# Copies and additions that free PSUM banks go first at the borders of blocks, two groups of weight sums are issued a step earlier, and v gets four places

## The chip, the cores and the metric

The kernel runs on one core of a Trainium2 chip. The metric is the device time of one execution in microseconds. Engines are named as in the profile: PE (TensorE, matmuls), ACT (ScalarE), DVE (VectorE), POOL (GpSimd) and SP (SyncE, which issues the DMAs). Each engine works through its own instructions in the order in which they were issued, and an instruction that waits holds back all behind it on that engine.

## The reference

```python
scores = scale * np.matmul(q_c, k_c.transpose(0, 1, 2, 4, 3))     # chunks of 64 tokens, heads of 64
attn = softmax(scores); x = np.matmul(attn, v_c)                  # 4608 tokens x 512
h = x @ w_in                                                      # MoE 1: 512 -> 2048
x = (h * (1.0 / (1.0 + np.exp(-h)))) @ w_out                      # 2048 -> 512
h = x @ w_in2                                                     # MoE 2: 512 -> 1024
solu = h * softmax(h)
ln = (solu - mean(solu)) / np.sqrt(var(solu) + 1e-06) * g_ln
out = ln @ w_out2                                                 # 1024 -> 512
```

## The kernel before

The 4608 tokens are worked in nine blocks of 512 (b = 0 to 8). All matmuls are in fp16; each fp32 value is carried as a high and a low half. `split` makes them: the high half on ACT (L113), the low half on DVE (L118) or POOL (L117). A product of two such values takes three matmuls.

Blocks 0 and 1 multiply plainly. From block 2 on (FAST = 2) a product of two matrices is done with seven products instead of eight, over sums of quarters: `h_fast` is the first product of MoE 1, `x_fast` the second, `m_fast` the first of MoE 2. All three run through `combine`, which holds partial results in PSUM (tiles pa, pb, pc) and moves them out: the copy of j = 0 on ACT (L529, into h[0], which is called hc, xc or e by the user), of j = 3 (L533), of j = 1 (L536), and additions on DVE (L569: j = 4 from pc, j = 2 from pa, j = 6 from pb). The last product (j = 5) goes into pa again, once the addition of j = 2 has read it. `h_fast` runs two halves, i = 0 and 1, interleaved, then two more, i = 2 and 3. There are eight PSUM banks, which all tiles share: a tile's first matmul waits until the last reader of the bank's former tile is done.

The sums of weights that the seven products need are made while blocks 1 and 2 run: `w1_sums` and `w2_sums` in block 1, `w3_sums` in block 2. A group is eight matmuls into wq, two ACT copies (L420, L421), four DVE sums (L423 to L426) and four splits on ACT and POOL into the staging tile ws; those of w1 and w2 go to DRAM by SP.

The order of the work around is set by hand. `step(s)` puts between the eight parts of a block's second product what the next block's attention needs: scores of one tile in steps 0, 1, 3 and 4, the product with v in steps 3 to 6, and groups of weight sums in the steps that W2F (w2's four groups, block 1) and W3S (w3's two groups, block 2) name. Attention of a tile is: qk loaded, split into qbh, qbl and kb (high halves on ACT), scores s_ps, maximum am, exponentials ae, transposed weights pT by DMA, v split into vbh and vbl, product x_ps, copy xf (L342).

At a border of blocks, `m_norm` makes the input u of the last product from e: exponentials (L799, L801), squares (L807), scaling (L817), u's high half on ACT (L818) and its low half on DVE (L821). This runs beside the next block's `h_fast`. In `combine` the list `behind` already puts a few instructions behind the copy L536 of i = 1:

```python
                i = A.activation(h[1], a, AF.Copy).ins
                while before:
                    tc.add_manual_dep(before.pop(), i.name, ORDERED, reason="copy first")
```

Of the kernel before, what the change touches and what calls it, by code (L numbers as in the profile page):

```python
# [46 lines left out]
def fused(ctx: ExitStack, tc: tile.TileContext, qkv, w1, w2, w3, w4, g_ln, out):  # L47
# [16 lines left out]
    MO = (0, 1, 2, 3)  # L64
    W3S = [0, 3]
    W1F = [3, 5, 7, 9, 11, 13, 14, 15]
    W2F = [3, 1, 7, 3]
    EXB = [6, 7, 10, 13, 14]
# [115 lines left out]
    def load_v(t):  # L184
        if t is not None:
            n = ORDER.index(t % TPB) if t // TPB > FAST else 0
            tag = ("vs", "h4", "h5", "h6")[n]
            vs[t] = one.tile([P, 512], F32, tag=tag, name="vs")
            nc.sync.dma_start(out=vs[t], in_=qkv[t, :, 2])

    def prep_qk(t, eng_l=G, ahead=True):
        q_, k_ = (y.rearrange("p (s i) -> p s i", s=NS) for y in qk.pop(t))
        qbh, qbl = qbs[t] if t in qbs else qb
        kb = one.tile([P, 2, NS, CH], F16, tag="xb2" if t in qbs else "k", name="kb")
        for r in (lo, hi):
            split(qbh[r, :, r], qbl[r, :, r], q_[r], 1.0, A, eng_l)
        split(kb[:, 0], kb[:, 1], k_, 1.0, A, V if t // TPB > FAST else eng_l)
        kt[t] = (qbh, qbl, kb[:, 0], kb[:, 1])
        if ahead and t % TPB != ORDER[-1]:
            load_qk(after(t))  # L200

    def prep_v(t):
        v = vs.pop(t).rearrange("p (s i) -> p s i", s=NS)
        vh, vl = vbh, vbl
        for r in (lo, hi):
            ready[1] = split(vh[r, :, r], vl[r, :, r], v[r], S_V, A, V)
        vt[t] = (vh, vl)
        if t // TPB <= FAST:
            load_v(after(t))
# [39 lines left out]
    def a_pv(t):  # L249
# [15 lines left out]
        if t % TPB != ORDER[-1]:  # L265
            prep_v(after(t))
        if o == ORDER[2]:
            v_done[:] = ready
        x_keep(b, o, ps.rearrange("p k c i -> p k (c i)"), S_X / (S_V * S_P))
        if sums_of and o == ORDER[2]:  # L270
            with tc.issue_after(v_done[0]), tc.issue_after(v_done[1]):
                sums_of.pop()()

    sums_of, v_done = [], [None, None]


# [57 lines left out]
    def x_keep(b, o, ps, scale):  # L334
# [5 lines left out]
        c = slice(o % 2 * P, o % 2 * P + P)  # L340
        f = one.tile([P, KD, P], F32, tag="h7" if o == ORDER[2] and b > FAST else f"h{o // 2}", name="xf")
        A.activation(f, ps, AF.Copy, scale=scale)  # L342
# [6 lines left out]
        split(xb[b, 2][:, 0, :, c], xb[b, 2][:, 1, :, c], f[:, 2:4], 1.0, A, G)  # L349
        if o == ORDER[1] and b > FAST:  # L350
            sums_of.append(lambda: x_sums(b, o, c, f))
        else:
            x_sums(b, o, c, f)

    def x_sums(b, o, c, f):
# [7 lines left out]
        for i in range(2):  # L363
            y = x.rearrange("p h t k n -> p h (t k) n")[:, :, 4 * i:4 * i + 4, c]
            split(y[:, 0], y[:, 1], t[i].rearrange("p t k n -> p (t k) n"), 1.0, A, V)


# [74 lines left out]
    def w1_sums(p):  # L442
# [3 lines left out]
        def staging():  # L446
# [4 lines left out]
             lambda j: w1s[p // 2][j, :, p % 2], [y[:, i] for i in range(4)], staging,  # L451
             y[:, 0::3].rearrange("p n a b -> p n (a b)"))

    def w2_sums(c, q):
# [61 lines left out]
    ORDERED = mybir.DependencyInfo(mybir.DependencyClass.NoSync, mybir.DependencyReason.DATA)  # L516
    behind = []

    def combine(h, shape, seq, product, done, add, c21_first=False, before=()):

# [5 lines left out]
        for j in seq:  # L526
            if j == 0:
                product(j, a, True)
                A.activation(h[0], a, AF.Copy)  # L529
            elif j == 3:  # L530
# [3 lines left out]
            elif j == 1:  # L534
                product(j, a, False)
                i = A.activation(h[1], a, AF.Copy).ins  # L536
                while before:
                    tc.add_manual_dep(before.pop(), i.name, ORDERED, reason="copy first")
            elif j == 4:
                p = bank(shape, "pc")  # L540
                product(j, p, True)
                add(0, h[0], p)
                done(0, 0, h[0])
# [24 lines left out]
    def plain_add(n, y, p):  # L568
        V.tensor_tensor(out=y, in0=p, in1=y, op=ALU.add)  # L569

# [8 lines left out]
    def h_fast(b, i):  # L579
# [7 lines left out]
        def done(r, c, x):  # L587
# [14 lines left out]
            else:  # L602
# [4 lines left out]
        yield from combine(h, [P, 2, HB], HSEQ, lambda *a: h_product(b, *a), done, plain_add,  # L607
                           before=behind if i == 1 else ())

# [14 lines left out]
    def x_fast(b, step, beside):  # L624
# [3 lines left out]
        def product(j, ps, start):  # L628
            step(XSEQ.index(j))
            if held:  # L630
                with tc.issue_after(v_done[0]), tc.issue_after(v_done[1]):
                    quarter(1, 1, held.pop())
# [91 lines left out]
    def m_fast(b, c, alt=False):  # L724
# [40 lines left out]

        yield from combine(y, [P, 512], XSEQ, product, done, add)
        u_tags, uT_tags = ["m1", "w3_10"], [tags[0] if c else "m2", tags[1]]
# [7 lines left out]
    def m_norm(b, ts, parts, m, es, u_tags, uT_tags, eng_l=V, defer=0):  # L775
# [39 lines left out]
        for i in range(n):  # L815
            e, u = es[i], us_[i]
            V.tensor_scalar(out=e, in0=e, scalar1=nmu[:, i:i + 1], scalar2=c[:, i:i + 1], op0=ALU.add, op1=ALU.mult)  # L817
            i_ = A.activation(u[:, 0, :], e, AF.Copy).ins  # L818
            if n > 1 and not defer and more_(b):
                behind.append(i_)  # L820
            eng_l.tensor_tensor(out=u[:, 1, :], in0=e, in1=u[:, 0, :], op=ALU.subtract)  # L821
            if isinstance(uT_tags[i], str):
# [144 lines left out]
    for b in range(NB):  # L967
# [46 lines left out]
        def step(s):  # L1014
# [10 lines left out]
            if b and s == 1:  # L1025
                run(m_out(b - 1, MO[TPB - 1]))
            for i in VL.get(s, ()) if b >= FAST else ():
                load_v(m + ORDER[i] if i < TPB else after(m + ORDER[-1]))
# [83 lines left out]
```

## Time and profile before

| | us |
|---|---|
| median of 3 runs | 1175.66 (1175.33 to 1175.7) |
| the profiled execution | 1176.06 |
| its span, first to last instruction | 1174.3 |
| PE busy | 1126.9 (96%) |
| DVE busy | 916.4 (78%) |
| ACT busy | 806.2 (69%) |
| POOL busy | 250.1 (21%) |

The profile is that of one execution. PE is busy almost all the time, the granted clock of its core is 0.991 of full speed, and the matmuls fill 1126.9 us. What can be changed without another set of matmuls is the time in which PE waits.

### The profile page before, as it was taken

Reading aid. Unit: us, or ns where it says so; the run is one execution under the profiler, and the core shown is the slowest. Engines: PE = TensorE matmul, PEld = TensorE weight load, DVE = VectorE, ACT = ScalarE, POOL = GpSimd, SP = SyncE. Lnnn points to the kernel's source line nnn. Section 1 sums busy time; section 2 is a strip of 40 time slices with the busy share of each in tenths; the row PEclk is TensorE's granted clock in tenths of the full one; section 3 lists DMA queues with packets and bytes.
Section 4 is the critical chain, followed back from the end, with each engine's and each line's share of the span. In section 5 each row is a group of like instructions: output and inputs, shape, how many; then the busy total and the mean of one; then the engine's idle time right before and its main releaser. Section 6 shows DMA issues by size and latency. Waiting matters only on the chain.

```text
span 1174.3 us, 23559 instructions
## 1 busy us (share of the span) xinstructions
PE 1126.9 (96%) x9036; PEld 769.2 (66%) x9036; DVE 916.4 (78%) x1638; ACT 806.2 (69%) x1475; POOL 250.1 (21%) x243
## 2 busy tenths in 40 slices
PE   6998898988999999999999999999999999999998
PEld 5444344444657866787678767876787777777853
DVE  5999998487588797789878986898689868886453
ACT  6887678766567767856875687568756876577253
POOL 2655434334201520031003100310021002100001
PEclk8999999999999999999999999999999999999999
DMA  6657579543446655776577567756776677565604
GB/s 261 224 179 208 152 232 270 163 140 112 143 127 203 197 151 144 189 233 180 154 189 234 171 153 198 225 171 162 187 218 181 162 176 217 175 162 145 204 21 116
DMA packets 205169, 209.18 MB, mean 178 GB/s; under 512 B 120192, under 2 KB 130432, under 8 KB 205056
## 3 DMA queue, kind: packets, MB, share of 16 engines
q1 hardware_dynamic: 205056, 207.68, 61.4%
q8 instruction: 70, 1.15, 0.4%
q14 instruction: 43, 0.35, 0.1%
HBM read 156.24 MB, written 24.12 MB: 154 GB/s over the span
## 4 chain that ended last, share of the span: by engine, by line
PE 61%; DVE 14%; ACT 11%; DMA 5%; issue 5%; POOL 3%; SPq 0%; ACTq 0%; POOLq 0%; DVEq 0%
PE o_ps L858 4%; PE o_ps L850 4%; PE o_ps L851 4%; PE pa L620 4%; PE pa L619 4%; PE pa L618 4%; PE pa L511 3%; PE pa L513 3%; PE pa L512 3%; PE pa L745 2%; PE pa L743 2%; PE pa L744 2%; DVE vbl L118 2%; PE pb L620 2%; PE pb L618 2%
## 5 line engine op out<-in xcount | busy, mean ns | idle before, releaser
L113 ACT ACTIVATE q<-hc 128x512 f16<-128x512 f32 x196 | 120.5, 627 | 43.1 <-DVE hc L598 16.0
L118 DVE SCALAR_TENSOR_TENSOR q<-hc,q 128x512 f16<-128x512 f32 x196 | 138.2, 721 | 10.9 <-ACT q L113 8.7
L117 POOL TENSOR_TENSOR qbl<-qk,qbh 64x512 f16<-64x512 f32 x54 | 71.4, 1322 | 265.7 <-ACT qbh L113 224.8
L618 PE MATMUL pa<-q,ring 128*128 128x256 f16 x448 | 122.1, 273 | 0.0
L620 PE MATMUL pa<-q,ring 128*128 128x256 f16 x448 | 122.1, 273 | 0.0
L619 PE MATMUL pa<-q,ring 128*128 128x256 f16 x448 | 122.1, 273 | 0.0
L850 PE MATMUL o_ps<-w4h,uT 128*128 128x512 f16 x288 | 109.1, 379 | 0.4 <-DVE e L801 0.4
L851 PE MATMUL o_ps<-w4l,uT 128*128 128x512 f16 x288 | 109.1, 379 | 0.0
L814 POOL TENSOR_TENSOR c<-c,mhalf 128x2 f32<-128x2 f32 (+1 forms) x22 | 14.1, 640 | 387.3 <-DVE c L813 377.4
L512 PEld LDWEIGHTS <-ring 128*128 128x128 f16 x784 | 76.7, 98 | 17.7 <-issue 7.4
L619 PEld LDWEIGHTS <-ring 128*128 128x128 f16 x784 | 76.7, 98 | 11.1
L618 PEld LDWEIGHTS <-ring 128*128 128x128 f16 x784 | 76.7, 98 | 11.1
L511 PEld LDWEIGHTS <-ring 128*128 128x128 f16 x784 | 76.7, 98 | 10.7 <-DMA ring<-w1s 0.4
L513 PEld LDWEIGHTS <-ring 128*128 128x128 f16 x784 | 76.7, 98 | 8.9
L620 PEld LDWEIGHTS <-ring 128*128 128x128 f16 x784 | 76.7, 98 | 8.9
L858 PE MATMUL o_ps<-w4h,uT 128*128 128x512 f16 x288 | 70.1, 379 | 0.0
L511 PE MATMUL pa<-xb,ring 128*128 128x256 f16 x224 | 61.0, 272 | 3.0 <-DVE hc L569 3.0
L511 PE MATMUL pa<-x,ring 128*128 128x256 f16 x224 | 61.0, 272 | 3.0 <-ACT hc L529 2.4
L511 PE MATMUL pb<-x,ring 128*128 128x256 f16 x224 | 61.1, 273 | 0.1
L618 PE MATMUL pb<-q,ring 128*128 128x256 f16 x224 | 61.1, 273 | 0.0
L619 PE MATMUL pb<-q,ring 128*128 128x256 f16 x224 | 61.1, 273 | 0.0
L620 PE MATMUL pb<-q,ring 128*128 128x256 f16 x224 | 61.1, 273 | 0.0
(277 smaller groups left out, 3490.8 us busy)
## 6 DMA issues: line engine op xcount, KB each, us to landing
ring<-w1s SPq DMA_DIRECT2D x196, 256.0 KB, 3.2
ring<-w2s SPq DMA_DIRECT2D x196, 256.0 KB, 3.7
wst<-w SPq DMA_DIRECT2D x48, 512.0 KB, 4.0
qk<-qkv SPq DMA_DIRECT2D x29, 512.0 KB, 4.1
vs<-qkv SPq DMA_DIRECT2D x36, 256.0 KB, 3.1
out<-o SPq DMA_DIRECT2D x36, 256.0 KB, 2.3
w1s<-ws SPq DMA_DIRECT2D x32, 128.0 KB, 2.1
w2s<-ws SPq DMA_DIRECT2D x16, 256.0 KB, 2.0
```

The lines of the kernel that those rows point to most:

```text
L113: ready[0] = A.activation(dst_h, src, AF.Copy, scale=scale).ins
L117: return G.tensor_tensor(out=dst_l, in0=src, in1=dst_h, op=ALU.subtract).ins
L118: return V.scalar_tensor_tensor(out=dst_l, in0=src, scalar=scale, in1=dst_h, op0=ALU.mult, op1=ALU.subtract).ins
L511: T.matmul(ps[:, c], wh, x[:, 0, k], start=first, stop=False, skip_group_check=True)
L512: T.matmul(ps[:, c], wh, x[:, 1, k], start=False, stop=False, skip_group_check=True)
L513: T.matmul(ps[:, c], wl, x[:, 0, k], start=False, stop=k == 1, skip_group_check=True)
L618: T.matmul(ps[:, c], wh, g[:, 0], start=first, stop=False, skip_group_check=True)
L619: T.matmul(ps[:, c], wh, g[:, 1], start=False, stop=False, skip_group_check=True)
L620: T.matmul(ps[:, c], wl, g[:, 0], start=False, stop=q == 1 and f == 3, skip_group_check=True)
L850: T.matmul(ps, uh[:, k], w4h[:, k, :], start=k == 0, stop=False)
L851: T.matmul(ps, uh[:, k], w4l[:, k, :], start=False, stop=False)
L858: T.matmul(ps, ul[:, k], w4h[:, k, :], start=False, stop=k == K2 - 1)
```

## The change

It adds no operation and takes none away; it moves some in their engines' order.

1. W3S: the second group of w3's sums is issued in step 2 of block 2 rather than in step 3. W2F: of the two groups of w2's sums in step 3 of block 1, one is issued in step 2.
2. The tiles of v that block 1 loads use four places (vs, h4, h5, h6) instead of one, and are loaded at the steps in VL. The sums of block 2's own x are put behind v's splits, as in later blocks.
3. `behind` becomes five lists. "keys": the last staging copy of w1's sums goes behind kb's high half. "first" and "second": in block 2, instructions of m_norm for block 1 go behind the copies L529 and L536 of i = 1. "sum": u's low halves go behind the addition L569 of j = 4, i = 1, at all borders. "joined": from block 3 on the high halves of the last tile's x differences go behind the copy of e from pa (L529) in `m_fast`.

```diff
-    W3S = [0, 3]
+    W3S = [0, 2]
-    W2F = [3, 1, 7, 3]
+    W2F = [2, 1, 7, 3]
...
-            n = ORDER.index(t % TPB) if t // TPB > FAST else 0
+            n = ORDER.index(t % TPB) if t // TPB >= FAST else 0
...
         split(kb[:, 0], kb[:, 1], k_, 1.0, A, V if t // TPB > FAST else eng_l)
+        put_behind("keys", ready[0])
...
             split(y[:, 0], y[:, 1], t[i].rearrange("p t k n -> p (t k) n"), 1.0, A, V)
+            if o == ORDER[3] and b > FAST:
+                behind["joined"].append(ready[0])
...
+        if p == 7:
+            behind["keys"].append(ready[0])
...
-    behind = []
-
-    def combine(h, shape, seq, product, done, add, c21_first=False, before=()):
+    behind = {n: [] for n in ("first", "second", "sum", "joined", "keys")}
+
+    def put_behind(name, i):
+        while behind.get(name):
+            tc.add_manual_dep(behind[name].pop(), i.name, ORDERED, reason="put behind")
+
+    def combine(h, shape, seq, product, done, add, c21_first=False, names=(None, None, None)):
...
-                A.activation(h[0], a, AF.Copy)
+                put_behind(names[0], A.activation(h[0], a, AF.Copy).ins)
...
-                i = A.activation(h[1], a, AF.Copy).ins
-                while before:
-                    tc.add_manual_dep(before.pop(), i.name, ORDERED, reason="copy first")
+                put_behind(names[1], A.activation(h[1], a, AF.Copy).ins)
...
-                add(0, h[0], p)
+                i = add(0, h[0], p)
+                if names[2]:
+                    put_behind(names[2], i)
...
-                           before=behind if i == 1 else ())
+                           names=("first", "second", "sum") if i % 2 else (None, None, None))
...
-        yield from combine(y, [P, 512], XSEQ, product, done, add)
+        yield from combine(y, [P, 512], XSEQ, product, done, add, names=(None if c else "joined", None, None))
...
-            i_ = A.activation(u[:, 0, :], e, AF.Copy).ins
+            high = A.activation(u[:, 0, :], e, AF.Copy).ins
+            low = eng_l.tensor_tensor(out=u[:, 1, :], in0=e, in1=u[:, 0, :], op=ALU.subtract).ins
             if n > 1 and not defer and more_(b):
-                behind.append(i_)
-            eng_l.tensor_tensor(out=u[:, 1, :], in0=e, in1=u[:, 0, :], op=ALU.subtract)
+                behind["second"].append(high)
+                behind["sum"].append(low)
+            elif n == 1 and b == FAST - 1 and ts[0] == 1:
+                behind["first"].extend(exps[-np:])
+                behind["second"].append(high)
+                behind["sum"].append(low)
+            elif n == 1 and b == FAST - 1 and ts[0] != 2:
+                behind["first"].append(high)
...
-            for i in VL.get(s, ()) if b >= FAST else ():
+            for i in VL.get(s, ()) if b >= FAST - 1 else ():
```

The order of instructions shows what this moves. Lines of the changed kernel carry higher numbers there: L585 is L569 of before, L606 is L590 (silu), L834 and L835 are L818 and L821. The numbers behind names tell tiles apart; hc0 of i = 0 is hc0_8486, of i = 1 hc0_8506.

DVE at one of the borders between blocks from 2 on, before:

```order
L569 TENSOR_TENSOR hc0_8486<-pc_8588,hc0_8486 128x512
L821 TENSOR_TENSOR u_8453<-e_8328,u_8453 128x1024
L821 TENSOR_TENSOR u_8454<-e_8329,u_8454 128x1024
L569 TENSOR_TENSOR hc0_8506<-pc_8607,hc0_8506 128x512
L118 SCALAR_TENSOR_TENSOR q_8418<-hc0_8486,q_8418 128x512
L569 TENSOR_TENSOR hc3_8489<-pa_8490,hc3_8489 128x512
L569 TENSOR_TENSOR hc3_8509<-pa_8510,hc3_8509 128x512
```

and after the change:

```order
L585 TENSOR_TENSOR hc0_8486<-pc_8588,hc0_8486 128x512
L585 TENSOR_TENSOR hc0_8506<-pc_8607,hc0_8506 128x512
L835 TENSOR_TENSOR u_8453<-e_8328,u_8453 128x1024
L835 TENSOR_TENSOR u_8454<-e_8329,u_8454 128x1024
L118 SCALAR_TENSOR_TENSOR q_8418<-hc0_8486,q_8418 128x512
L118 SCALAR_TENSOR_TENSOR q_8418<-hc0_8506,q_8418 128x512
L585 TENSOR_TENSOR hc3_8489<-pa_8490,hc3_8489 128x512
```

The second addition from pc now stands ahead of u's two low halves, and the low half of q for i = 1 ahead of the two additions from pa.

ACT at the same border, from the loading of the table for silu (L590), before:

```order
L590 ACT_TABLE_LOAD
L590 ACTIVATE hc0_8486<-hc0_8486 128x512
L113 ACTIVATE q_8418<-hc0_8486 128x512
L590 ACTIVATE hc0_8506<-hc0_8506 128x512
L113 ACTIVATE q_8418<-hc0_8506 128x512
L590 ACTIVATE hc3_8489<-hc3_8489 128x512
```

and after:

```order
L606 ACT_TABLE_LOAD
L606 ACTIVATE hc0_8486<-hc0_8486 128x512
L606 ACTIVATE hc0_8506<-hc0_8506 128x512
L113 ACTIVATE q_8418<-hc0_8486 128x512
L113 ACTIVATE q_8418<-hc0_8506 128x512
L606 ACTIVATE hc3_8489<-hc3_8489 128x512
```

The silu of i = 1 now stands ahead of the high half of q for i = 0.

ACT in block 2 at steps 2 to 4, behind the exponentials of step 1's tile (xc1 is x_fast's copy of j = 1, vbh the split of v), before:

```order
L113 ACTIVATE x2q_4510<-xc0_4216 128x2x128
L536 ACTIVATE xc1_4217<-pa_4220 128x512
L113 ACTIVATE qbh_113<-qk_4443 64x8x64 x2
L228 ACTIVATE ae_4600,as_4601<-s_ps_4573,am_4598 128x64 x8
L113 ACTIVATE kb_4611<-qk_4443 128x512
L113 ACTIVATE vbh_115<-vs_4394 64x8x64 x2
L342 ACTIVATE xf_4659<-x_ps_4630 128x512
```

and after:

```order
L430 ACTIVATE y_4515<-wq_4517 128x512
L113 ACTIVATE x2q_4510<-xc0_4216 128x2x128
L431 ACTIVATE y_4516<-wq_4518 128x512
L113 ACTIVATE w3s_4277<-y_4516 128x512
L113 ACTIVATE w3s_4278<-y_4516 128x512
L113 ACTIVATE w3s_4276<-y_4515 128x512
L113 ACTIVATE w3s_4279<-y_4515 128x512
L552 ACTIVATE xc1_4217<-pa_4220 128x512
L113 ACTIVATE qbh_113<-qk_4443 64x8x64 x2
L229 ACTIVATE ae_4628,as_4629<-s_ps_4601,am_4626 128x64 x8
L113 ACTIVATE kb_4639<-qk_4443 128x512
L113 ACTIVATE vbh_115<-vs_4394 64x8x64 x2
```

Two copies of wq and four splits into w3s stand ahead of qbh, the exponentials and kb.

## Rows read from the trace of the kernel before

**Rows 1.** The page's busy part: engine, us, share of the span, instructions.

```profile
PE 1126.9 (96%) x9036; PEld 769.2 (66%) x9036; DVE 916.4 (78%) x1638; ACT 806.2 (69%) x1475; POOL 250.1 (21%) x243
```

**Rows 2.** PE's waits: line, tile awaited, us in total, times, longest.

```profile
PE pa L511 <- DVE hc L569: 3.0, 5, 0.7
PE pa L743 <- ACT e L529: 1.4, 2, 0.7
```

**Rows 3.** DVE's timeline in one border: start us, us, line, operation [idle <-releaser].

```profile
681.23 1.54 DVE L817 TENSOR_SCALAR e<-e,nmu,c 128x1024 f32<-128x1024 f32 x2 [0.87 <-POOL c L814]
682.68 0.68 DVE L569 TENSOR_TENSOR hc<-pc,hc 128x512 f32<-128x512 f32 x1
683.29 2.35 DVE L821 TENSOR_TENSOR u<-e,u 128x1024 f16<-128x1024 f32 x2
685.55 0.69 DVE L569 TENSOR_TENSOR hc<-pc,hc 128x512 f32<-128x512 f32 x1
686.78 0.69 DVE L118 SCALAR_TENSOR_TENSOR q<-hc,q 128x512 f16<-128x512 f32 x1 [0.54 <-ACT q L113]
687.39 1.28 DVE L569 TENSOR_TENSOR hc<-pa,hc 128x512 f32<-128x512 f32 x2
```

**Rows 4.** ACT's timeline in the same border.

```profile
684.16 1.28 ACT L590 ACT_TABLE_LOAD   x1
685.46 0.63 ACT L590 ACTIVATE hc<-hc 128x512 f32<-128x512 f32 x1
686.12 0.63 ACT L113 ACTIVATE q<-hc 128x512 f16<-128x512 f32 x1
686.65 0.61 ACT L590 ACTIVATE hc<-hc 128x512 f32<-128x512 f32 x1
```

**Rows 5.** PE's timeline: the last product's start in this border and the last.

```profile
688.13 0.27 PE L511 MATMUL pa<-xb,ring 128*128 128x256 f16 x1 [0.72 <-DVE hc L569]
...
1044.33 0.27 PE L511 MATMUL pa<-xb,ring 128*128 128x256 f16 x1
```

**Rows 6.** Timelines of ACT and PE in block 1, at step 1's kb.

```profile
236.98 0.42 ACT L113 ACTIVATE ws<-y 128x256 f16<-128x256 f32 x1 [2.15 <-DMA w1s<-ws]
...
238.75 0.19 PE L217 MATMUL s_ps<-kb,qbh 128*128 128x64 f16 x1 [1.32 <-ACT kb L113]
239.54 0.19 PE L218 MATMUL s_ps<-kb,qbh 128*128 128x64 f16 x1 [0.61 <-DVE kb L118]
```

**Rows 7.** Timelines of PE, DVE and POOL in block 1, steps 3 to 5.

```profile
258.03 0.38 PE L411 MATMUL wq<-w2t,ident 128*128 128x512 f16 x1 [1.37 <-ACT xf L342]
...
274.15 0.20 PE L264 MATMUL x_ps<-pT,vbl 128*128 128x64 f16 x1 [2.84 <-DVE vbl L118]
...
272.44 1.65 DVE L118 SCALAR_TENSOR_TENSOR vbl<-vs,vbh 64x512 f16<-64x512 f32 x1
...
250.36 5.74 POOL L117 TENSOR_TENSOR ws<-y,ws 128x512 f16<-128x512 f32 x4 [12.22 <-ACT ws L113]
```

**Rows 8.** Timelines of PE and DVE at the opening of block 2.

```profile
313.34 0.27 PE L511 MATMUL pa<-x,ring 128*128 128x256 f16 x1 [1.94 <-ACT hc L529]
...
319.28 0.27 PE L511 MATMUL pa<-x,ring 128*128 128x256 f16 x1 [0.53 <-ACT hc L536]
...
322.42 1.29 DVE L118 SCALAR_TENSOR_TENSOR q<-hc,q 128x512 f16<-128x512 f32 x2
```

**Rows 9.** Timelines in block 2: DVE, POOL, ACT (first and last of 8), PE.

```profile
385.89 2.65 DVE L425 TENSOR_TENSOR y<-y 128x512 f32<-128x512 f32 x1
...
386.84 1.15 POOL L117 TENSOR_TENSOR w3s<-y,w3s 128x512 f16<-128x512 f32 x1
...
390.74 0.30 ACT L228 ACTIVATE ae<-s_ps,am 128x64 f32<-128x64 f32 x1
...
392.76 0.34 ACT L228 ACTIVATE ae<-s_ps,am 128x64 f32<-128x64 f32 x1
...
403.40 0.19 PE L217 MATMUL s_ps<-kb,qbh 128*128 128x64 f16 x1
```

More of the change, by code (lines that the diff above doesn't have):

```diff
@@ L1 @@
-from contextlib import ExitStack
+from contextlib import ExitStack, contextmanager
 import concourse.bass as bass
@@ L207, in prep_v @@
         vt[t] = (vh, vl)
-        if t // TPB <= FAST:
+        if t // TPB < FAST:
             load_v(after(t))
@@ L266, in a_pv @@
             prep_v(after(t))
-        if o == ORDER[2]:
             v_done[:] = ready
@@ L270, in a_pv, with behind_v @@
         if sums_of and o == ORDER[2]:
-            with tc.issue_after(v_done[0]), tc.issue_after(v_done[1]):
+            with behind_v():
                 sums_of.pop()()
     sums_of, v_done = [], [None, None]
+    @contextmanager
+    def behind_v(on=True):
+        if on:
+            with tc.issue_after(v_done[0]), tc.issue_after(v_done[1]):
+                yield
+        else:
+            yield
     def f_scores(t, y):
@@ L340, in x_keep @@
         c = slice(o % 2 * P, o % 2 * P + P)
-        f = one.tile([P, KD, P], F32, tag="h7" if o == ORDER[2] and b > FAST else f"h{o // 2}", name="xf")
+        f = one.tile([P, KD, P], F32, tag="h7" if o == ORDER[2] else f"h{o // 2}", name="xf")
         A.activation(f, ps, AF.Copy, scale=scale)
@@ L349, in x_keep @@
         split(xb[b, 2][:, 0, :, c], xb[b, 2][:, 1, :, c], f[:, 2:4], 1.0, A, G)
-        if o == ORDER[1] and b > FAST:
+        if o == ORDER[1]:
             sums_of.append(lambda: x_sums(b, o, c, f))
@@ L568, in plain_add @@
     def plain_add(n, y, p):
-        V.tensor_tensor(out=y, in0=p, in1=y, op=ALU.add)
+        return V.tensor_tensor(out=y, in0=p, in1=y, op=ALU.add).ins
     qt = {}
@@ L630, in product @@
             if held:
-                with tc.issue_after(v_done[0]), tc.issue_after(v_done[1]):
+                with behind_v():
                     quarter(1, 1, held.pop())
```

## The prediction

> **What bounds the kernel now.** I read the page's busy part first: TensorE (PE) is busy for 1126.9 of 1174.3 us [rows 1]. The matmuls are the same before and after, so the change can only move the other 47.4 us, in which PE waits. The table of PE's waits says for what. Most of it lies in the opening, block 0 and the tail, which the change does not touch. What it does touch are the waits for a PSUM bank, or for an operand, at seven kinds of places; the largest group is five times the addition L569 at a block's border, 3.0 us together, and the copy of e counts 1.4 us [rows 2]. Then I read the timelines of DVE, ACT and PE around each of these places, and set the rows of the order before and after against them. Waits that the change could remove add up to about 15 us: those of rows 2 and 5 to 8, and some tenths beside them.
>
> **The borders from block 2 to 8 (six of them).** In the border at 681 us, DVE scales two tiles of e (L817), adds i = 0 of pc, makes the two low halves of u (2.35 us), adds i = 1 of pc, waits 0.54 us for ACT's high half of q, makes the low half of q for i = 0, and only then adds pa (687.39, two of them in 1.28) [rows 3]. PE's last product accumulates in that pa, so it starts at 688.13, 0.72 after it could have [rows 5]. What released it was the first addition of pa. Ahead of that stands the low half of q, which waits for ACT: table load until 685.46, silu, high half of q, silu, high half of q [rows 4].
>
> The change puts the second pc addition before the two low halves of u. This makes the second silu's input early, and it is also why the order then changes further down: on ACT both silus stand before both high halves of q, and on DVE both low halves of q stand before the first addition of pa. That is two low halves ahead of it instead of one. Step by step: the silus start at 685.46 and, at the 0.53 spacing of two unrelated ACT instructions (686.12 to 686.65), at 685.99; the high halves start at 686.52 and 687.05 and end at 687.15 and 687.68 [rows 4]. DVE has finished the u's at 682.68 + 2 x 0.61 + 2.35 = 686.25, so it is idle again; its low halves start at 687.18 and, 0.61 later, 687.78, and the addition of pa at 688.39 instead of 687.39 [rows 3]. So each border costs 1.0 us more, not 0.7 less. The earlier pc additions free a bank that nobody waits for. Five borders have this wait [rows 2]; at the last PE starts the product at 1044.33 without one [rows 5], so some of the 1.0 is covered there, and I take off 0.2. Sum: 5 x 1.0 + 0.8 = **+5.8**. Bounds: -3.0 (all five waits vanish) and +6.5.
>
> **The copy of kb in block 1 ("keys").** ACT had an instruction in between that waited 2.15 us for a DMA (the staging copy of w1's last sum) and ended at 237.40; the second half of qbh and kb stood behind it. PE waited for kb's high half 1.32 and its low half 0.61 [rows 6]. Both now stand ahead of it. The load they need has long landed, since the first half ran before the wait; kb comes 2 us earlier. What is late next, the staging copy, is wanted only by stores. **-1.9**; bounds -1.9 and -1.2 (the low half still waits).
>
> **Block 1: a group of w2's sums from step 3 to 2, v in four places.** Before, two groups stood in step 3; their matmuls waited 1.37 for a bank whose copy was behind qbh, kb and vbh on ACT, and later PE waited 2.84 for the low half of v, which DVE made in 1.65 while POOL ran [rows 7]. The moved group finds its banks free. But its copies and sums now stand on ACT and DVE ahead of the next tile's qbh, kb and vbh, and its tiles are those of the group before, whose four POOL splits end at 256.10 [rows 7]. So one y copy waits until then, and I estimate the third group's matmuls 1.2 late, kb's low half at about 262.7 (needed at 263.3) and v's at 264.8 (0.8 late). By the place of the 2.84 wait the tile of v is split earlier, and without the second group's sums between, at 272.5 to 273.5 instead of 274.09; the transposed weights behind it come about 1.5 us earlier. I take **-1.5**. Bounds: -4.2 (both waits of rows 7 vanish) and +1.5 (two of the moved group's DVE sums take 1.65 instead of 0.69 and v gains nothing).
>
> **Block 2's opening (u of block 1).** The copy of h for i = 1 goes ahead of the exponentials: the wait of 1.94 goes, and that of 0.53 too [rows 8]. But DVE now has the two low halves of q (322.42, 1.29 for two) ahead of the second pa addition. They are tied to ACT's table load, so this addition ends at about 323.5, where PE, 2.5 earlier by the two waits, would ask for it at about 322.0. Net 2.5 - 1.5: **-1.0**; bounds -2.5 and 0. The later half of the block has one such wait of 0.5; I take **-0.3**.
>
> **Block 2: w3's second group from step 3 to 2.** Its two y copies and four splits now stand on ACT ahead of qbh, the exponentials and kb of the tile whose scores PE reaches at 403.40 [rows 9]. ACT is free of the exponentials before them at 393.1. Then, at 0.6 a copy and 0.6 a DVE sum: two y copies with another one between them until about 395.0, DVE's four sums (one operation of the softmax before and one between them) until about 398.9, last split 399.6, copy 400.2, qbh 401.4, eight exponentials (2.4, as from 390.74 to 393.10) 403.8, kb 404.4, its low half 405.6. That is 2.2 late at 403.40, and v's low half, behind it, costs 1.6 more. PE's later waits up to the e copy (1.3 together) vanish in that slack: +2.5. One row speaks for more: the same kind of sum took 2.65 us at 385.89, and ended 0.55 after POOL's operation that ran from 386.84 to 387.99; such a wait here gives +3.4. [...] I keep **+2.5**, since where POOL stands is my estimate. Bounds: -0.7 (nothing late, the small waits go) and +3.4.
>
> **"joined".** The copy of e goes ahead of the high halves of x on ACT. Two waits, 1.4 us [rows 2]; the first lies behind the new slack of block 2, the second goes: **-0.7**; bounds -1.4 and 0. The x halves are late by one copy of 0.6 and wait for DVE's differences anyway.
>
> **Sum** against the profiled execution: +5.8 - 1.9 - 1.5 - 1.0 - 0.3 + 2.5 - 0.7 = +2.9. It took 1176.06 us, so 1179.0; the median of the runs is 0.4 lower, so **1178.5**, +0.24%. About 0.2% (2.3 us) is what a measurement of this kernel can tell from no change.
>
> **Rivals.**
> A: the borders get what the names say. If the second high half of q, or its input, is ready early enough for DVE to pass both low halves before PE is done with pb, the waits vanish: -3.0 instead of +5.8, so 1169.7. For it: the pc addition is indeed 2.3 earlier. Against: ACT's table load, not that addition, sets the time of the high halves. It decides once the addition of pa starts before 686.5. 0.15.
> B: w3's group is hidden. If DVE's sums run in the gaps before 397, kb is in time: -0.7 and the first e wait goes too, so about 1174.7, no change. For it: ACT idles there before. Against: its queue is in order, and each split waits for a DVE sum. 0.27.
> C: the moved w2 group costs instead of gaining, +1.5: 1181.5. For it: eight POOL splits now follow each other. Against: v's earlier splits. 0.18.
> The forecast: 0.36; the rest 0.04.
>
> **How the numbers follow.** A and a few mixed cases are faster: 0.18. B, and the part of the forecast whose w2 and opening terms come out at their better ends, lie within 0.2%: 0.36. The rest of the forecast and C are slower: 0.46. The forecast's own range is 1175.5 to 1181.5; with C and most of A it is 1170 to 1183.
>
> **What would show it.** PE's table of waits: pa for the pc/pa addition at borders near 1.7 each, six of them (right), or none (A). kb's wait at 238.75 gone. In block 2 a wait of about 2 us at the scores of step 4 for kb's low half, and v's behind it (right), or none (B). The v wait at step 5 of block 1 under 2.8. Block 2's opening with no wait for the copy L529, but one of about 1.5 for an addition. The prediction is wrong if the borders' waits shrink, or if block 2 shows no new wait.

## The result, and the profile after

The changed kernel takes 1184.61 us, the median of 5 runs (1183.5 to 1185.81). The kernel before took 1175.7 us beside it (5 runs, 1175.33 to 1177.01). The ratio is 1.0076, with an interval from 1.0061 to 1.009: slower, by 8.9 us. The profiled execution took 1184.49 us, its span 1182.7.

The page of the changed kernel, first its busy part, which answers to [rows 1]; then, from the table of PE's waits, line, tile awaited, us in total, times, longest, which answer to [rows 2]:

```profile
PE 1126.4 (95%) x9036; PEld 768.5 (65%) x9036; DVE 917.0 (78%) x1638; ACT 803.4 (68%) x1475; POOL 250.2 (21%) x243
```

```profile
PE pa L523 <- DVE hc L585: 9.8, 7, 1.7
PE x_ps L265 <- DVE vbl L118: 6.8, 5, 2.1
...
PE x_ps L263 <- ACT vbh L113: 3.6, 3, 2.3
```

Every engine does what it did; the 8.4 us by which the span is longer are PE's waits and, as the windows below show, some matmuls at half clock. The largest group is the one that the change was to shorten: the wait for the additions L585 (L569 of before) has gone from 3.0 us to 9.8.

To place the loss I took the start of each of PE's 9036 matmuls in one trace minus the start of the same one in the other, and read where the difference changes. Minus is gained. The column of the prediction is its terms.

| place | predicted | measured |
|---|---|---|
| up to 237 us, where the order is the same | 0 | -1.0 |
| "keys", 237 to 241 us | -1.9 | -0.4 |
| block 1, w2's group and v, 241 to 290 | -1.5 | +2.1 |
| opening of block 2, 312 to 330 | -1.0 | -1.4 |
| second half of block 2's opening, to 403 | -0.3 | +0.1 |
| block 2, w3's group, 403 to 430 | +2.5 | +3.3 |
| six borders | +5.8 | +5.7 |
| "joined" | -0.7 | -0.5 |
| rest, in pieces of 0.35 and less | 0 | +0.5 |
| sum | +2.9 | +8.4 |

The first line is no part of the change: among the kernels below, whose order is the same there, this stretch ended up to 1.9 us apart from one profiled execution to the next.

**A border after.** The border of [rows 3 to 5], now at 694 us. Timelines of DVE, ACT and PE (start us, us, engine, line, operation, idle before and its releaser):

```profile
688.38 0.68 DVE L585 TENSOR_TENSOR hc<-pc,hc 128x512 f32<-128x512 f32 x1
688.98 2.35 DVE L835 TENSOR_TENSOR u<-e,u 128x1024 f16<-128x1024 f32 x2
692.26 1.29 DVE L118 SCALAR_TENSOR_TENSOR q<-hc,q 128x512 f16<-128x512 f32 x2 [0.93 <-ACT q L113]
693.47 1.28 DVE L585 TENSOR_TENSOR hc<-pa,hc 128x512 f32<-128x512 f32 x2
```

```profile
689.26 1.28 ACT L606 ACT_TABLE_LOAD   x1
690.55 1.15 ACT L606 ACTIVATE hc<-hc 128x512 f32<-128x512 f32 x2
691.61 1.13 ACT L113 ACTIVATE q<-hc 128x512 f16<-128x512 f32 x2
```

```profile
694.20 0.27 PE L523 MATMUL pa<-xb,ring 128*128 128x256 f16 x1 [1.50 <-DVE hc L585]
```

Behind the table load stand two silus, two high halves of q, and on DVE two low halves; only then comes the first addition of pa, 2.93 us after the table load's end. Before it was 1.95 (687.39 less 685.44). PE waits 1.50 instead of 0.72; at the last border, at 1052.56 us, 0.64 instead of nothing.

**Block 2 after**, at the place of [rows 9]: PE's waits in the timeline.

```profile
404.37 0.19 PE L218 MATMUL s_ps<-kb,qbh 128*128 128x64 f16 x1 [1.40 <-ACT kb L113]
405.62 0.19 PE L219 MATMUL s_ps<-kb,qbh 128*128 128x64 f16 x1 [1.06 <-DVE kb L118]
408.23 0.24 PE L265 MATMUL x_ps<-pT,vbl 128*128 128x64 f16 x1 [1.73 <-DVE vbl L118]
```

DVE there, a sum of the moved group and kb's low half:

```profile
397.04 1.15 DVE L435 TENSOR_TENSOR y<-y 128x512 f32<-128x512 f32 x1
...
404.88 0.68 DVE L118 SCALAR_TENSOR_TENSOR kb<-qk,kb 128x512 f16<-128x512 f32 x1
```

**Block 1 after**, at the places of [rows 6, 7]. Timelines of PE, DVE, POOL and ACT:

```profile
238.13 0.19 PE L219 MATMUL s_ps<-kb,qbh 128*128 128x64 f16 x1 [1.45 <-DVE kb L118]
...
264.12 0.20 PE L265 MATMUL x_ps<-pT,vbl 128*128 128x64 f16 x1 [1.10 <-DVE vbl L118]
...
272.43 0.20 PE L263 MATMUL x_ps<-pT,vbh 128*128 128x64 f16 x1 [2.32 <-ACT vbh L113]
...
274.80 0.23 PE L265 MATMUL x_ps<-pT,vbl 128*128 128x64 f16 x1 [2.13 <-DVE vbl L118]
```

```profile
237.39 0.69 DVE L118 SCALAR_TENSOR_TENSOR kb<-qk,kb 128x512 f16<-128x512 f32 x1
...
266.59 1.59 DVE L244 TENSOR_TENSOR ae<-ae 128x512 f16<-128x512 f32 x1
268.11 1.64 DVE L435 TENSOR_TENSOR y<-y 128x512 f32<-128x512 f32 x1
269.85 0.69 DVE L436 TENSOR_TENSOR y<-wq,y 128x512 f32<-128x512 f32 x1
...
271.76 1.54 DVE L118 SCALAR_TENSOR_TENSOR vbl<-vs,vbh 64x512 f16<-64x512 f32 x1
```

```profile
266.48 2.72 POOL L117 TENSOR_TENSOR ws<-y,ws 128x512 f16<-128x512 f32 x2 [0.81 <-ACT ws L113]
270.49 2.27 POOL L117 TENSOR_TENSOR ws<-y,ws 128x512 f16<-128x512 f32 x2 [1.29 <-ACT ws L113]
```

```profile
269.78 0.63 ACT L113 ACTIVATE ws<-y 128x512 f16<-128x512 f32 x1 [1.97 <-DVE y L435]
...
271.11 1.26 ACT L113 ACTIVATE vbh<-vs 64x512 f16<-64x512 f32 x2
```

kb's high half is in time, its low half is 1.45 late. The wait of 1.37 for a bank has gone, but in its place come 1.10, 2.32 and 2.13 for v, where 2.84 stood before. Three DVE instructions of 0.68 to 0.69 us took 1.54 to 1.64 while POOL made splits. One of them is a sum, L435; ACT waited 1.97 for it with a split of that sum, and v's high half stood behind, at 271.11 (268.60 before). The kernel before has the same hold some 5 us earlier (L243 and L425 are the L244 and L435 of the changed kernel). DVE and ACT there:

```profile
261.89 1.59 DVE L243 TENSOR_TENSOR ae<-ae 128x512 f16<-128x512 f32 x1
263.42 1.64 DVE L425 TENSOR_TENSOR y<-y 128x512 f32<-128x512 f32 x1
```

```profile
265.09 0.63 ACT L113 ACTIVATE ws<-y 128x512 f16<-128x512 f32 x1 [2.46 <-DVE y L425]
...
268.60 1.27 ACT L113 ACTIVATE vbh<-vs 64x512 f16<-64x512 f32 x2
```

**The clock.** Windows of the changed kernel: start and end, length, busy time and instructions of the five engines, the granted clock as a share of full speed, DMA share, GB/s.

```profile
272.40:274.80 2.40, 0.24 (x3) 0.12 (x3) 2.34 (x4) 1.64 (x3) 1.02 (x2) 0.98 0.56 219
274.80:278.20 3.40, 3.40 (x28) 2.02 (x29) 2.60 (x6) 1.51 (x3) 0.00 (x0) 0.51 0.02 5
...
404.30:408.20 3.90, 1.08 (x26) 0.86 (x25) 3.84 (x6) 2.94 (x7) 1.53 (x2) 0.95 0.02 5
408.20:411.20 3.00, 2.97 (x31) 2.48 (x32) 2.32 (x4) 1.58 (x3) 0.51 (x1) 0.50 0.76 175
```

In both places PE was idle for most of the window ahead (busy 0.24 of 2.40 us, 1.08 of 3.90), and then ran at half clock (0.51 and 0.50 granted) for 3.40 and 3.00 us; in the stretches behind (278.20 to 282.10 and 411.20 to 415.00 us) the granted clock is 1.00 again. By the same difference of starts this cost 1.6 us in block 1 and 1.4 in block 2. So of the 2.1 us that block 1's place lost, the waits account for 0.5. The kernel before has 1.00 at both places:

```profile
274.10:278.00 3.90, 3.85 (x37) 2.13 (x38) 3.85 (x8) 1.09 (x3) 1.89 (x2) 1.00 0.47 149
403.40:408.00 4.60, 4.45 (x77) 4.03 (x75) 4.25 (x8) 3.75 (x9) 3.90 (x4) 1.00 0.60 146
```

### The profile page after: what moved, and what is told of

It is laid out like the page before. It is cut to its first block, busy times and chain, and to the rows that moved or that the text cites. A ratio compares the mean times of both kernels' runs of the same rounds, so it can differ in the third digit from the quotient of the medians.

```text
span 1182.7 us, 23562 instructions
## 1 busy us (share of the span) xinstructions
PE 1126.4 (95%) x9036; PEld 768.5 (65%) x9036; DVE 917.0 (78%) x1638; ACT 803.4 (68%) x1475; POOL 250.2 (21%) x243
## 3 DMA queue, kind: packets, MB, share of 16 engines
q8 instruction: 70, 1.15, 0.4%
## 4 chain that ended last, share of the span: by engine, by line
PE 61%; DVE 15%; ACT 10%; issue 6%; DMA 4%; POOL 3%; SPq 0%; ACTq 0%; POOLq 0%; DVEq 0%
PE o_ps L873 4%; PE o_ps L881 4%; PE o_ps L874 4%; PE pa L635 4%; PE pa L634 4%; PE pa L636 4%; PE pa L523 3%; PE pa L525 3%; PE pa L524 3%; PE pa L761 2%; PE pa L760 2%; PE pa L759 2%; PE pb L636 2%; PE pb L635 2%; PE pb L634 2%
## 5 line engine op out<-in xcount | busy, mean ns | idle before, releaser
L830 POOL TENSOR_TENSOR c<-c,mhalf 128x2 f32<-128x2 f32 (+1 forms) x22 | 14.1, 640 | 393.6 <-DVE c L829 383.7
L523 PE MATMUL pb<-x,ring 128*128 128x256 f16 x224 | 61.1, 273 | 0.0
L525 PE MATMUL pb<-x,ring 128*128 128x256 f16 x224 | 61.1, 273 | 0.0
L524 PE MATMUL pb<-x,ring 128*128 128x256 f16 x224 | 61.1, 273 | 0.0
L634 PE MATMUL pb<-q,ring 128*128 128x256 f16 x224 | 61.1, 273 | 0.0
```

The source lines that it names most:

```text
L523: T.matmul(ps[:, c], wh, x[:, 0, k], start=first, stop=False, skip_group_check=True)
L524: T.matmul(ps[:, c], wh, x[:, 1, k], start=False, stop=False, skip_group_check=True)
L525: T.matmul(ps[:, c], wl, x[:, 0, k], start=False, stop=k == 1, skip_group_check=True)
L634: T.matmul(ps[:, c], wh, g[:, 0], start=first, stop=False, skip_group_check=True)
```

## The experiments

Each kernel was timed beside the kernel before. Its ratio is to that kernel. The theory is that the borders lose because DVE makes two low halves of q ahead of the addition of pa, and that w3's and w2's moved groups lose by operands made late; its rivals are that the borders lose by something else that the change moved there, and that the moved groups are hidden.

**1. u's low halves where they were.** The changed kernel without "sum" at the borders from block 2 on:

```diff
                 behind["second"].append(high)
-                behind["sum"].append(low)
```

> The changed kernel without one of its parts: at the borders from block 2 on, u's low halves are no longer put behind the second addition from pc; everything else stays. Theory (that part lets the second low half of q go ahead of the first addition from pa, 1.0 us a border): the six waits for an addition at the borders, 1.5 to 1.7 us each in the changed kernel (0.64 at the last), fall to 0.5 to 0.7 (none at the last), and the time falls by 5.8 from 1184.6 to about 1178.8. Rival (the borders' waits come from the copy of e and the x halves that 'joined' moves, or from the later arrival of the chain): they stay near 1.5 and the time stays within 1 us of 1184.6.

Measured: 1179.27 us (1177.93 to 1179.86), ratio 1.0033 [1.002, 1.0046]. Measured against the kernel before of each session, that takes the loss from 8.9 to 4.0 us. The waits for an addition at the borders are five again, 2.4 us together and 0.6 at most, and the difference of starts no longer grows there. The borders lose through this one list.

**2. w3's second group back in step 3.**

```diff
-    W3S = [0, 2]
+    W3S = [0, 3]
```

> The changed kernel with w3's second group back in step 3 of block 2. Theory (its copies and splits on ACT hold back qbh, the exponentials and kb of the next tile): the waits for kb and v's low half at 404 to 408 us (4.2 us together) vanish, the small ones of the kernel before come back (0.7), the wait for the copy of e stays away because of 'joined', and the time falls by about 4.0 to 1180.6. Rival (what is late there is late for another reason, such as the qk load): the time stays within 1 us of 1184.6.

Measured: 1180.91 us (1179.13 to 1182.62), ratio 1.0049 [1.0036, 1.0062]; the loss goes from 8.9 to 5.7. The three waits at 404 to 408 us are gone. From 400 to 430 us the changed kernel falls back by 3.3 us against this one. The group is not hidden: the rival falls.

**3. w2's moved group back in step 3.**

```diff
-    W2F = [2, 1, 7, 3]
+    W2F = [3, 1, 7, 3]
```

> The changed kernel with the moved group of w2's sums back in step 3 of block 1; v keeps its four places and the copy of kb stays first. Theory (the moved group's copies, sums and POOL splits hold back the next tile's attention, and the group behind it then collides with v's split): the waits at 264, 272 and 275 us (5.5 us together) turn back into those of the kernel before (1.4, 0.4 and 2.8), and the time falls by 2 to 3 us to about 1182. Rival (v's four places, which put loads of v ahead of stores in SP's queue, or the sums of x moved behind v, are to blame): the waits at 272 and 275 stay and the time stays within 1 us of 1184.6.

Measured: 1184.12 us (1183.64 to 1185.6), ratio 1.0078 [1.0066, 1.009]: no gain in the time. In the trace the place itself is 2.7 us better than in the changed kernel (1.6 of it is the half clock, which this kernel does not have there: 1.00 from 272 to 282 us), but other places took it back:

```profile
273.29 0.20 PE L265 MATMUL x_ps<-pT,vbl 128*128 128x64 f16 x1 [2.84 <-DVE vbl L118]
...
363.27 0.28 PE L523 MATMUL pa<-xb,ring 128*128 128x256 f16 x1 [1.37 <-DMA ring<-w1s]
```

The first is the wait of [rows 7]; the other one of those rows is back too, 1.47 at 257.19. So the waits follow the group, and the rival falls: v keeps its four places here. The second, for a load of w1's sums, is new: in experiment 1 it was 1.16, in experiment 8 it was 2.42, and in the other kernels 0.52 or less. Some 0.5 each went at the opening and at w3. The place's loss is real, but the time of the whole kernel did not show it here.

**4. The addition of pa first.** The changed kernel, and at the borders to block 3 and later the low halves of q for j = 0 go behind the addition of pa for i = 1:

```diff
-                add(3, h[3], a)
+                i = add(3, h[3], a)
+                if names[2]:
+                    put_behind("low", i)
...
-            split(y[:, 0], y[:, 1], x, S_G, A, V)
+            low = split(y[:, 0], y[:, 1], x, S_G, A, V)
+            if j == 0 and b > FAST and i < 2:
+                behind["low"].append(low)
```

> The changed kernel with one thing more: at the borders from block 2 on, the low halves of q for the first quarter (i = 0 and 1) are put behind the addition from pa of i = 1 on DVE. Theory (the place of the two low halves of q ahead of the additions from pa is the whole of the borders' cost): both additions from pa run right behind u's low halves, at about 5.0 and 5.6 us after the scaling of e starts, before PE asks for them at 6.0; all six waits at the borders vanish (8.5 us together), and the time falls to about 1176.3. Rival (u's low halves behind the second pc addition, or ACT's later high halves, cost by themselves): waits of 0.5 to 1 us stay at the borders, or come back as waits for q in the second product.

Measured: 1176.38 us (12 runs, 1173.24 to 1179.73), ratio 1.0008 [0.9997, 1.0018]. DVE's timeline at the border:

```profile
685.19 2.35 DVE L839 TENSOR_TENSOR u<-e,u 128x1024 f16<-128x1024 f32 x2
687.45 1.28 DVE L587 TENSOR_TENSOR hc<-pa,hc 128x512 f32<-128x512 f32 x2
688.65 1.28 DVE L118 SCALAR_TENSOR_TENSOR q<-hc,q 128x512 f16<-128x512 f32 x2
```

The addition of pa now follows u directly, without the idle 0.93 and the 1.29 of q's low halves. All six border waits are gone. u's low halves stay behind the second addition of pc here, as in the changed kernel, so the order between pa and q's low halves is what the borders lost by. The five waits of the kernel before, 3.0 us together, are gone with them. That the earlier additions from pc pay for any of this is not shown, since no run has the new order without them: in [rows 3] DVE had ended the second addition from pc at 686.24 and stood idle until 686.78, so with q's low half behind them the additions from pa could have come before PE's request at 687.41 there as well.

**5. The same, with both groups back** (experiments 2 to 4 together).

> The kernel of e4_pa_first with both moved groups of weight sums back (w2's in step 3 of block 1, w3's in step 3 of block 2); the first copies at the opening, kb first, 'joined' and v's four places stay. Theory (the costs of the parts add up): 3.7 less for w3's group, 0.5 to 2.6 less for w2's, so 1170 to 1172, faster than both the kernel before (1175.2) and the changed one. Rival (what is gained is given back at the next place, as seemed to happen where w2's group was put back): no lower than 1173.5.

Measured: 1169.99 us (1168.66 to 1172.25), ratio 0.9955 [0.9941, 0.9969]: faster than both kernels, at the lower end of what the theory had; the rival's 1173.5 is above all five runs.

**6. Experiment 5 with w2's group moved again** (W2F = [2, 1, 7, 3]).

> As e5_best, but w2's group in step 2 of block 1, as the change has it. One theory, from the trace of e3_w2_back at the place itself: 2.6 us more than e5_best, and the difference is still there at the end. The other, from the run times of e3_w2_back: at most 0.5 us more, since PE, when earlier, waits later for a load into the ring of weights or for block 2's chain.

Measured: 1170.95 us (1169.52 to 1173.51), ratio 0.9963 [0.995, 0.9976]. The intervals overlap; in the traces the moved group costs 1.5 us between 241 and 290 us, where the granted clock was below full in both: 0.84 over 275.50 to 281.90 us here, 0.63 over 272.80 to 276.80 us in experiment 5.

**7. The opening too.** In experiment 5 the low halves of q are put behind the addition of pa in block 2 as well:

```diff
-            if j == 0 and b > FAST and i < 2:
+            if j == 0 and b >= FAST and i < 2:
```

> As e5_best, and at the opening of block 2 too the low halves of q (first quarter, i = 0 and 1) are put behind the addition from pa of i = 1. Theory (the wait of 1.3 to 1.6 us for that addition at 322 to 324 us is due to the two low halves ahead of it): it vanishes and the time falls by 1.3 to 1.5. Rival (the addition is held by u's low half or by the copies): at least 0.7 of the wait stays.

Measured: 1169.67 us (1168.86 to 1171.48), ratio 0.995 [0.9938, 0.9963]. The wait of 1.29 at the opening vanished, and the time stayed. Where it went, in PE's timeline and in a window of this kernel:

```profile
349.07 0.27 PE L523 MATMUL pa<-x,ring 128*128 128x256 f16 x1 [2.13 <-ACT hc L545]
```

```profile
349.00:356.00 7.00, 6.93 (x49) 5.58 (x49) 2.73 (x3) 5.31 (x9) 0.42 (x1) 0.76 0.69 191
```

PE came to the next wait earlier, so that wait grew from 0.78 to 2.13; behind it the granted clock was 0.76 on average over 7 us. The copy L545 it waits for stood on ACT behind a square (L827) that had waited until 347.26 for DVE's means.

**8. v in one place again.** Experiment 5 without v's four places and with the sums of block 2's x where they were:

```diff
-            n = ORDER.index(t % TPB) if t // TPB >= FAST else 0
+            n = ORDER.index(t % TPB) if t // TPB > FAST else 0
...
-            for i in VL.get(s, ()) if b >= FAST - 1 else ():
+            for i in VL.get(s, ()) if b >= FAST else ():
```

> As e5_best, but v's tiles of block 1's loads in one place, loaded as in the kernel before, and the sums of block 2's own x issued as before. Theory (v's four places take away only the waits at step 6 of block 1): waits of 1.0 and 0.3 come back near 281 us, and the time is 1.0 to 1.3 above e5_best. Rival (the four places cost something elsewhere, by loads that stand ahead of stores in SP's queue): the same time or less.

Measured: 1171.22 us (1170.14 to 1171.31), ratio 0.9958 [0.9944, 0.9971]. Against 1169.99 the intervals overlap. The trace has the two waits that v's places had taken away (1.17 at 277.67, 0.52 at 278.41), and no half clock ahead of them (1.00 from 271.00 to 276.40 us); but also a wait of 2.42 for the load at 363.66, so the difference can't be put down to v alone. Inconclusive in size.

**9. Copies ahead of the square, and kb's low half ahead of a subtraction.** Experiment 7, with two further lists:

```diff
+            if n == 1 and b == FAST - 1 and ts[0] == 3:
+                behind["first"].append(sq)
...
+            if t == FAST * TPB + ORDER[0]:
+                behind["kb"].append(sub)
...
+        put_behind("kb", low)
```

Here sq is the square of the last tile (L827) and sub the subtraction of the maximum (L231) in step 0's tile; kb's low half is what sub is put behind.

> As e7_opening, with two things more. In block 1 the subtraction of the maximum (ae of the tile before) is put behind the low half of kb on DVE: theory (it is the subtraction that stands between the two low halves of qb and holds kb's low half, so that the copy of kb on ACT gained so little), the wait of about 1.0 for kb's low half falls to about 0.35; rival (the two low halves of qb hold it), it stays. In the later half of block 2's first product the copies of h (j = 0) are put ahead of the squares of tile 3's u on ACT: theory (the 1.4 us that e7_opening gained at the opening were given back there, its wait for that copy being 2.13 instead of 0.78, because the squares wait for DVE's means), the wait vanishes and the gain of the opening shows: in all 2.7 below e5_best, about 1167.3. Rival (the next thing in the chain, the ring of weights or the last product's addition, takes it back): no lower than 1169.

Measured: 1166.24 us (4 runs, 1165.85 to 1167.04), ratio 0.9918 [0.9905, 0.9931]: the fastest of all. ACT's timeline (L548 is the copy L545 of experiment 7, L830 its square L827) and a window:

```profile
345.18 1.08 ACT L548 ACTIVATE hc<-pa 128x512 f32<-128x512 f32 x2
347.81 1.15 ACT L830 ACTIVATE u<-e,nmu 128x1024 f32<-128x1024 f32 x1 [1.55 <-DVE nmu L827]
```

```profile
347.30:353.00 5.70, 5.49 (x51) 4.78 (x50) 2.41 (x7) 3.84 (x7) 0.55 (x1) 1.00 0.88 276
```

The copies run ahead of the square, the wait of 2.13 at 349 is gone, and the clock stays at 1.00, until 364 us as well: against experiment 7, 3.6 us from 345 to 360 us. The rival's 1169 is above all four runs. The wait for kb's low half is 0.89 instead of the 1.00 of experiment 5, and the difference of starts changes by 0.1 there: this part gained next to nothing. The trace of this kernel also loses 1.0 us against experiment 5 between 241 and 290 us, with a granted clock of 0.76 from 273 to 280 us where that one had 0.80; whether the moved subtraction is behind that is not shown.

**10. POOL made to wait.** Experiment 6, in which the four POOL splits of w2's third group wait until v's low half of step 5 is made:

```diff
+        if t == FAST * TPB + ORDER[2]:
+            for i in lows:
+                tc.add_manual_dep(i, ready[1].name, WAIT, reason="POOL waits")
```

> As e6_best_w2_moved, but POOL's four splits of w2's third group wait until the low half of v at step 5 of block 1 is made. Theory (the moved group is dear because those splits and DVE's operations with two SBUF inputs hold each other up: three DVE operations took 1.5 to 1.65 us instead of 0.7 between 266 and 273 us in the changed kernel): these three fall to 0.7, v's low half is made 2 to 2.7 us earlier, the two waits of 2.3 and 2.1 at 272 and 275 us come to 2 to 2.5 together, and the time is 1 to 2.5 us below e6_best_w2_moved (1171.0). Rival (v is late because its high half stands behind the group's splits on ACT): the DVE operations get short, but the waits and the time stay.

Measured: 1171.28 us (6 runs, 1168.64 to 1173.77), ratio 0.996 [0.9946, 0.9974]: no gain against experiment 6. The timelines of DVE and POOL:

```profile
267.01 0.68 DVE L247 TENSOR_TENSOR ae<-ae 128x512 f16<-128x512 f32 x1
267.62 0.68 DVE L438 TENSOR_TENSOR y<-y 128x512 f32<-128x512 f32 x1
...
270.31 0.68 DVE L118 SCALAR_TENSOR_TENSOR vbl<-vs,vbh 64x512 f16<-64x512 f32 x1
...
277.11 2.72 DVE L118 SCALAR_TENSOR_TENSOR vbl<-vs,vbh 64x512 f16<-64x512 f32 x2
```

```profile
272.81 5.39 POOL L117 TENSOR_TENSOR ws<-y,ws 128x512 f16<-128x512 f32 x4
```

The three instructions that POOL had held (L247, L438 and vbl; L244, L435 and vbl in the changed kernel) now take 0.68 each. The waits of 2.32 and 2.13 shrink to 0.45 and 1.16, and the clock over 273.00 to 281.40 is 1.00. But the splits, now from 272.81 to 278.20, hold the next tile's softmax (an operation of 0.69 at 275.94 in the changed kernel took 1.36 here) and v's low halves instead, and PE waits 3.05 us at 281.42 for the transposed weights. Of the place's loss 0.9 us is saved, and the whole shows none of it. So POOL's hold on DVE is shown, by moving it; put here, it was paid again at the next tile.

## Why the prediction was wrong

It said slower, and it was; but the time, 1184.6, lies above the forecast's range, which ends at 1181.5, and above the wider one with the rivals, which ends at 1183. The profiled execution took 1184.49 us, 5.5 more than the sum's 1179.0. Of these 5.5, block 1's group and v make 3.6, "keys" 1.5 and w3's group 0.8; no other term is off by more than 0.5, and the stretch ahead of the change ran 1.0 shorter.

**The borders: right, in mechanism and size.** Predicted +5.8, measured +5.7. Each step is in the rows: the addition of pa starts 2.93 us after the table load's end instead of 1.95, 1.0 later; the waits are 1.57, 1.70, 1.50, 1.53, 1.56 and, at the last border, 0.64. Experiment 1 takes this loss away by leaving u's low halves where they were, experiment 4 by another order of pa and q. Rival A's gain was there to be had, since all six waits are gone in experiment 4; the order between those two instructions kept it out.

**w3's group: right in the working, too small by the clock.** Predicted +2.5. The chain came as written: four sums until 398.98 (predicted 398.9), last split 399.64 (399.6), kb's low half at 405.56 (405.6). The waits come to 4.35 us by the difference of starts, where I had 3.8, and 2.4 us were given back up to 430 us, more than the 1.3 that I counted: 1.4 at the small waits and 0.9 at the copy of e. What the sum lacked is the half clock (0.50) behind these waits, 1.4 us. From the 2.65 us that a sum took beside POOL at 385.89 [rows 9], the prediction had an estimate of +3.4 there by another cause, a sum held by POOL; the trace bears that out in part only, since the sum L435 at 397.04 took 1.15 beside POOL's splits, not 2.65. The measured +3.3 is near that estimate by luck.

**Block 1, w2's group and v: the failed step.** Predicted -1.5 from v's earlier splits, measured +2.1. The forecast had v's low half at 272.5 to 273.5, and the last of it came at 274.74. Two things were missing. First, the delay of one tile was not carried on to the group of sums behind it. The forecast itself had that tile's kb and v about 5.4 us later than before (262.7 and 264.8 against 257.37 and 259.36), and they came 4.7 later. The group left in step 3 stands behind that tile, and so its four sums came 4.7 later too: DVE made them from 265.06 to 270.54, right ahead of the next v, where the first of before's two groups in that step had them from 260.37 to 265.85. v's high half on ACT started at 271.11 instead of 268.60. POOL's hold is not what differs: in both kernels three instructions of 0.68 there took 2.7 to 2.8 us more, and ACT waited for the held sum before too (2.46), but that wait ended 3.5 us ahead of v's high half. In the changed kernel the held instructions stand in the chain that makes v. Experiment 10 shows it: with the splits elsewhere the same three take 0.68 each, v's high half starts at 269.66, and the waits of 2.32 and 2.13 become 0.45 and 1.16. For two held sums, rival C's mechanism, I had allowed +1.5 at the worst. Second, the half clock (0.51) behind two waits of 2.32 and 2.13, 1.6 us, stood in no bound; without it the place would be 0.5 us dearer than before. Experiments 3 and 6 confirm the sign at the place (2.7 and 1.5 us), though the whole shows 0 and 1.0.

**"Keys": the failed step of the smaller terms.** Predicted -1.9, bounds -1.9 to -1.2, measured -0.4. kb's high half came in time, but its low half stands on DVE behind two low halves of qb and a subtraction, and ends at 238.08, 0.69 after its start at 237.39. I had looked at ACT alone for what is late next, and named a copy that only stores want. Experiment 9 shows that taking the subtraction away is worth 0.1: ahead of the low half then still stand two low halves of qb.

**The opening, the second half and "joined"** came within 0.4 us of their terms: -1.4, +0.1 and -0.5. The wait predicted for an addition at about 323.5 is there, 1.28 at 323.82. The second half is near by luck: the wait of 0.49 at 353.75 went, as forecast, but one of 0.79 for another copy of j = 0 came at 352.03. It is the wait that grows in experiment 7 and goes in experiment 9.

Open stays why the clock fell at some waits and not at others of the same length: see below. The step of 8.9 us is also not the plain sum of its parts by medians: experiments 2, 3 and 4 took 3.2, 0.0 and 7.8 us off one by one, and 14.4 together. What makes the rest is not shown; the runs of experiment 4 alone lie 6.5 us apart.

## What to carry to other kernels

An instruction that is put earlier frees its successors too: follow the new order until the next instruction for which the bottleneck waits, since here two low halves went ahead of the one addition that mattered, and exchanging them was worth 8 us. A wait that goes may come back larger at the next instruction that had been late, so look at every engine for what is late next, and count the clock with it: behind waits of 4.2 and 4.5 us within a few us, matmuls at half clock (0.50 and 0.51) cost another 1.4 and 1.6 here. Test a part where it stands: the gain of one edit at its place (2.7 us) can be missing from the time of the whole kernel, when another wait behind it takes it back.

## What the runs showed of the hardware

**The clock fell after some of PE's waits and not after others.** The same wait, 2.84 or 2.85 us for v's low half, stands in five kernels: before, and in experiments 3, 5, 7 and 8. The window of the wait and the one behind it, in experiments 5 and 3:

```profile
270.00:272.80 2.80, 0.02 (x1) 0.00 (x0) 2.77 (x3) 1.73 (x4) 2.80 (x3) 0.92 0.24 94
272.80:276.80 4.00, 3.93 (x31) 2.27 (x32) 3.20 (x6) 1.74 (x3) 1.66 (x2) 0.63 0.36 134
```

```profile
270.40:273.20 2.80, 0.05 (x2) 0.00 (x0) 2.77 (x3) 1.75 (x4) 2.78 (x3) 1.00 0.24 94
273.20:277.20 4.00, 3.91 (x38) 2.15 (x39) 3.21 (x6) 1.71 (x3) 1.68 (x2) 1.00 0.36 135
```

With the same work ahead, experiment 5 went on at 0.63 and experiment 3 at 1.00. Experiment 7 slowed there too: from 273.25 to 274.94 its matmuls were spaced 0.43 us instead of 0.22. The kernel before (274.10 to 278.00) and experiment 8 (271.00 to 276.40) had 1.00. In experiment 9 a wait of 1.99 at the same place was followed by matmuls spaced 0.43 us instead of 0.22. Behind the two waits of 2.32 and 2.13 the clock fell in all five kernels that have them, the changed one (0.51 over 3.40 us) and experiments 1, 2, 4 and 6 (0.89 to 0.94 on average from 260 to 290 us, where experiment 3 had 1.00), and it fell behind the waits at w3's moved group in all four that have it there, the changed one (0.50 over 3.00 us) and experiments 1, 3 and 4 (0.77 on average from 400 to 415 us, where experiments 2, 6 and 7 had 1.00). What decides it where it came out either way is left open here.

**DVE's hold by POOL.** Beside POOL's splits three DVE instructions with two inputs in SBUF, L244, L435 and vbl, took 1.59, 1.64 and 1.54 us in the changed kernel; the same three took 0.68 each in experiment 10, with the splits elsewhere.
